# Weight loads of a two-branch kernel issued from ScalarE's DMA queue in place of SyncE's

## The chip, the cores and the metric

The kernel runs on one core of a Trainium2 chip. A core has TensorE for matmuls, VectorE (DVE), ScalarE (ACT) and GpSimd (POOL) for elementwise work, and SyncE (SP), which here only issues DMAs. Each engine takes its own instructions in order; engines wait for each other by semaphores. DMAs are issued as instructions of an engine's stream, here SyncE's and ScalarE's, and 16 DMA engines move the bytes. The metric is device microseconds of one execution.

## The reference

Both branches start from the same layer norm of x (2048 tokens of 448), and their sum is added to x:

```
xn = layernorm(x)
out = x + A(xn) + B(xn)
A: q, k, v = xn @ wqkv               (16 heads of 28)
   phi(t) = [softmax(t @ w_phi), softmax(-(t @ w_phi))]     for q and k, per head
   o = phi(q) @ (phi(k)^T v) / (phi(q) . sum(phi(k)) + 1e-6)
   A = o @ wo
B: h  = gelu(layernorm(xn) @ w1)     (448 columns in four groups)
   hs = [h shifted by 1, -1, 2, -2 tokens, group by group] @ w2
   x1 = xn + hs
   B  = x1 + gelu(layernorm(x1) @ w3) @ w4      (448 -> 1792 -> 448)
```

All tensors are bfloat16.

## The kernel before

Tokens are cut into 16 tiles of 128. The contraction of 448 is laid out in pieces of 64 rows, so that two matmuls run at once on the two row halves of TensorE.

The kernel is recorded as a flat list of operations. `Recorder.op` (L67) takes an engine, an output and inputs; `solve` (L76) derives from the order of the list which operation has to wait for which; `emit` (L152) writes one in-order stream for each engine. So the order of an engine's instructions is the order in which the list names them, and all operations have the lines of the recorder's helpers in the profile: L204 matmuls, L208 transposing matmuls, L212 ScalarE activations, L216 elementwise work, L219 transposing DMAs, L222 plain DMAs. `R.dma` (L221) and `R.dma_t` (L218) have SyncE as their default issuer.

The order is written by hand in two lists:

- A chain (L944 to L967) covers the front: layer norm of all tiles, its transposition to xnT, the V products (`ZV`), the w1 products with Gelu (`ZW`, `ZR`), the folding of w_phi into the q and k weights (`FO`), and the first pair of k, w2 and q products (`HF`). It interleaves matmuls of the two row halves; an entry `do(...)` is put into the list just where it stands, while the eviction belonging to a matmul group comes when the group's last matmul is placed.
- A play list (L1034 to L1057) covers the rest: k products with exponentials (`k0`, `k1`), q products (`q0`, `q1`), w2 products (`w0`, `w1_`), transpositions of the q exponentials (`T`) and of the second layer norm (`G`), the sum over keys (`K`), the w3 products with Gelu (`a`, `b`), the attention quotient (`N`) and the last products with w4 and wo (`f`), with stores (`S`).

The DMAs around the change are:

- `h_shift(0)` and `h_shift(1)` (L668): six copies each inside the tile hT, which put the shifted upper rows of h in place; w2 products read them.
- `rest_T(0)` and `rest_T(1)` (L665): transposition of the last 64 columns of h from hR (which shares its memory with gT, so the profile names it gT) to hRT. `rest_out` (L662) is the Gelu on ScalarE that writes hR.
- `load_w2` (L389): three DMAs, 336 KB and twice 56 KB. `load_w4` (L397): one of 1568 KB. `load_w3` (L394): two halves of 896 KB, called at two places. `wo_in` (L1030): two of 224 KB into the tile wv, which the V products have finished with by then. In the profile w1, w2, w3 and w4 are all named w.
- `q_T` (L706): 16 transpositions from hi, the q exponentials, to eqT. The lower eight land in eqT_lo, the upper eight in the memory of hT. `g_T` (L746): 16 transpositions from g_tok to gT.

ScalarE evicts most of PSUM in the front and all of the k and q exponentials (phik and hi) and the Gelus (hT, gT in the front; phik in the w3 stage, where h3T shares its memory). It changes its function table at the end of the front, before the first exponential, and again before the first Gelu of the w3 stage. At the start ScalarE's queue issues five loads, of x, wv and w1, beside SyncE's; at the end one store.

Of the kernel before, what the change touches and what calls it, by code (L numbers as in the profile page):

```python
# [6 lines left out]
ACT = mybir.ActivationFunctionType  # L7
# [217 lines left out]
def bass_parallel_sum__linear_kernel_hedgehog__mixer_s_mlp__prompt_kernel(  # L225
# [17 lines left out]
    with es:  # L243
# [249 lines left out]
        def fold(t, m, b, n):  # L493
            def side(k, hi):
                r, c0, c1 = (slice(64, CR), 2 * DH, CR) if hi else (slice(0, 64), 0, 3 * DH)
                return [(banks[b + k][:, CR * c + c0:CR * c + c1],
                         wT[r, t, c, START[m + k]:START[m + k] + 128], bd[r, CR * c + c0:CR * c + c1], n == 0 and c == 0)
                        for c in range(NC)]
            return side(n, 0), side(1 - n, 1)
# [24 lines left out]
        def xn_Td(i):  # L524
            R.dma_t(xnT[:, :, 128 * i:128 * i + 128], xn[:, i, :])
# [8 lines left out]
        def halves_of(first, second, start=False):  # L534
            return tuple([(out, lhs, rhs, start and n == 0) for n, (out, lhs, rhs) in enumerate(side)] for side in (first, second))
# [99 lines left out]
        def z_w1(g, m, b):  # L635
            def make(rows, kcs):
                lo, hi = rows
                return [(banks[b], w1[lo:hi, kc, 128 * m:128 * m + 128], xnT[lo:hi, kc, 512 * g:512 * g + 512],
                         rows == LO and n == 0) for n, kc in enumerate(kcs)]
            return make  # L640
# [230 lines left out]
        def play(fs):  # L871
            for f in fs:
                f[0](*f[1:])
# [18 lines left out]
        def do(f, *args):  # L892
            return "do", lambda: f(*args), ()
# [4 lines left out]
        def FO(t, m, n):  # L898
            return "both", fold(t, m, fb[t, m], n), ((fold_out, t, m, fb[t, m]),) if n else ()

        def XT(i, b, n=1, eng="ACT"):
            return "both", xn_T(i, b, n), ((xn_out, i, b, n, eng),)

        def XD(*t):
            return do(lambda: [xn_Td(i) for i in t])
# [4 lines left out]
        def ZV(i, *then):  # L910
            return "zip", z_v(i, vb[i]), then

        def ZW(g, m, *then):
            return "zip", z_w1(g, m, gb[g][m]), then
# [4 lines left out]
        def inside(n, job, inner):  # L919
            return (*job, (n, inner))  # L920

        def ZR(h, b, *then):
            return "zip", z_rest(h, b), then

        def EV(i, eng="ACT", n=1):
            return v_out, i, vb[i], eng, n

        def EW(g, m, n):
            return w1_out, g, m, gb[g][m], n
# [6 lines left out]
        def HF(p, n):  # L936
            then = ((), ((k_exp, 0, kq[0][0], 0), (k_exp, 0, kq[0][0], 1)), ((w2_out, 0, wb[0]),),
                    ((q_exp, 0, kq[0][1], 0), (q_exp, 0, kq[0][1], 1)))[(p + 1) * n]
            return "half", halves_of(*head[p][n], n == 0), then
# [20 lines left out]
            XT(8, 1, 1, "ACT"), ZW(3, 2, EW(3, 2, 1)), L(("r", 9, 1)), FO(1, 2, 0), L(("a", 10)), FO(1, 0, 1),  # L960
            ZW(3, 1, EW(3, 1, 1)), FO(1, 2, 1), ZV(12, EV(12, "DVE", 1)), ZV(8, EV(8, "DVE", 1)), L(("p", 9)),
            inside(3, ZR(0, 6, (rest_out, 0, 6), (rest_T, 0)), XT(9, 3, 1, "2")), FO(0, 2, 0),
            FO(0, 0, 0), XD(10), FO(0, 2, 1), FO(0, 0, 1), do(h_shift, 0), ZW(2, 2, EW(2, 2, 1)), do(load_w2),
            ZR(1, 5, (rest_out, 1, 5)), ZW(2, 1, EW(2, 1, 1)), ZV(11, EV(11, "ACT", 1)), ZV(10, EV(10, "ACT", 1)),
            ZW(2, 0, EW(2, 0, 1)), ZV(9, EV(9, "DVE", 1)), do(kv_picks), HF(0, 0), do(late_3), do(kv_ones), HF(1, 0), HF(2, 0),
            do(load_w4), do(h_shift, 1), do(rest_T, 1), HF(0, 1), do(load_w3, 0), HF(1, 1), HF(2, 1)], 400,
            "001010111100101001010010111010100")  # L967

        kp = [phi_pair(wpk, 2 * n, kq[n][0]) for n in range(8)]
# [53 lines left out]
        def f(n, k):  # L1023
            fp[k][n - 1]()
# [5 lines left out]
        def wo_in(eng="SP"):  # L1030
            load_lap(wo, A_wo, (eng, eng))

        K, G, S, T, kc, kb, W = kv_tile, g_T, store, q_T, kv_turn, kv_blocks, fin_tails
        play([  # L1034
            (w0, 2), (lo, 0), (kn, 0), (load_w3, 1), (k0, 1), (kx, 0), (k0, 2), (k1, 1), (w1_, 2), (q0, 1), (k1, 2),
            (q1, 1), (q0, 2), (T, 0), (k0, 3), (kn, 1), (q1, 2), (kn, 2), (T, 1), (lo, 1), (kx, 1), (kx, 2), (w0, 4),
            (k1, 3), (w1_, 4), (q0, 3), (k0, 4), (kn, 3), (q1, 3), (k1, 4), (w0, 6), (T, 3), (q0, 4), (w1_, 6),
            (lo, 3), (q1, 4), (kx, 3), (lo, 2), (sc, 0), (K, 0), (K, 1), (K, 2), (K, 3), (k0, 5), (q0, 5), (k1, 5),
# [2 lines left out]
            (A, 0), (lo, 6), (w1_, 10), (k1, 7), (kx, 4), (kx, 5), (lo, 4), (w0, 12), (lo, 5), (q0, 7), (w1_, 12),  # L1041
            (sc, 4), (lo, 11), (G, 0), (kn, 6), (A, 7), (AD, 4), (G, 2), (kn, 7), (A, 6), (T, 8), (lo, 10), (q1, 7),
            (a, 0), (w0, 14), (b, 0), (a, 1), (w1_, 14), (A, 5), (b, 1), (a, 2), (kx, 6), (K, 9), (K, 6), (a, 3),
            (wo_in,), (T, 10), (b, 2), (G, 6), (G, 4), (b, 3), (K, 13), (kx, 7), (lo, 9), (lo, 8), (G, 5), (K, 12),
            (K, 8), (K, 11), (lo, 15), (a, 4), (a, 5), (b, 4), (b, 5), (lo, 13), (K, 7), (K, 14), (lo, 14), (K, 15),
            (G, 7), (K, 10), (kc,), (sc, 8), (a, 6), (kb,), (T, 9), (a, 7), (A, 9), (b, 6), (A, 10), (N, 0), (b, 7),
            (f, 1, 0), (N, 1), (a, 9), (AD, 8), (AD, 11), (T, 11), (G, 11), (a, 8), (G, 9), (b, 9), (b, 8), (N, 2),
# [44 lines left out]
```

## Time and profile before

| | |
|---|---|
| three runs, median | 173.2 us (171.03 to 173.53) |
| profiled execution | 170.78 us, span of its instructions 169.1 us |
| DMA | 19.93 MB in 50567 packets, mean 118 GB/s |
| SyncE's DMA queue (q1) | 18.71 MB, 56.9% of the 16 engines' span |
| ScalarE's DMA queue (q10) | 0.89 MB, 1.6% |
| granted TensorE clock | 1.00 throughout |

The span runs from the first to the last instruction. "Busy" of TensorE is modelled for pipelined matmuls, so neighbouring matmuls overlap in the rows. A row of a timeline has the start, the length, the engine ("q" behind it for an instruction of its queue, a DMA issue), the line, the operation, the tiles (out<-in), the shapes and the count, and in brackets the idle time of the engine before it with what ended it. A row of DMA issues ends with the size and the time from issue to landing.

### The profile page before, as it was taken

To read this page: it belongs to the slowest core of one execution; us is meant where nothing else is said; L and a number is where in the kernel's file an instruction comes from. 1 tells how busy PE (TensorE), PEld (TensorE's weight loads), DVE (VectorE), ACT (ScalarE), POOL (GpSimd) and SP (SyncE) were. 2 spreads that over 40 slices of the span, in tenths; PEclk is the share of its full clock that TensorE was granted. 3 is DMA by queue.
4 is the path that set the end of the run, shared out by engine and by line. 5 is a ranking of instruction groups with operands and counts; after the bars stand their busy time and mean duration, and the time that the engine had idled before them with its cause. 6 is when DMAs were issued, how large, how long until landed. Compare 5 with 4: busy or idle time off the path is not lost.

```text
span 169.1 us, 5415 instructions
## 1 busy us (share of the span) xinstructions
PE 165.2 (98%) x2355; PEld 92.9 (55%) x2355; DVE 110.2 (65%) x250; ACT 79.4 (47%) x107; POOL 91.5 (54%) x125
## 2 busy tenths in 40 slices
PE   8899999999999999999999999999999999999994
PEld 7587679755455444445554555555455555444453
DVE  3889968149999989996692952876228656250131
ACT  3499873867997887555142422222042202504000
POOL 5578891003999999993645472272602717234040
PEclk9999999999999999999999999999999999999999
DMA  5995444699999959573026761467592113214011
GB/s 163 335 222 101 77 55 97 161 345 184 395 204 197 137 108 155 99 90 68 17 49 124 97 124 38 104 107 123 135 108 58 35 31 33 51 52 128 0 54 54
DMA packets 50567, 19.93 MB, mean 118 GB/s; under 512 B 41712, under 2 KB 49840, under 8 KB 50544
## 3 DMA queue, kind: packets, MB, share of 16 engines
q1 hardware_dynamic: 49424, 18.71, 56.9%
q10 hardware_dynamic: 1120, 0.89, 1.6%
q8 instruction: 18, 0.29, 0.7%
q14 instruction: 5, 0.04, 0.1%
HBM read 7.14 MB, written 1.84 MB: 53 GB/s over the span
## 4 chain that ended last, share of the span: by engine, by line
PE 98%; ACT 0%; DVE 0%; issue 0%
PE banks L204 96%; PE banks L208 1%; ACT xnT L212 0%; DVE vaug L216 0%; ACT rs L212 0%
## 5 line engine op out<-in xcount | busy, mean ns | idle before, releaser
L212 ACT ACTIVATE phik<-banks 128x1024 bf16<-128x1024 f32 (+1 forms) x44 | 41.7, 987 | 63.2 <-PE banks L204 63.2
L204 PE MATMUL banks<-gT,w 64*128 64x512 bf16 x392 | 47.1, 376 | 0.0
L204 PE MATMUL banks<-w,phik 64*128 64x448 bf16 (+3 forms) x434 | 45.2, 343 | 0.0
L216 DVE TENSOR_TENSOR vaug<-banks,vaug 128x464 f32<-128x464 f32 (+3 forms) x65 | 32.6, 511 | 19.2 <-PE banks L204 17.5
L216 POOL TENSOR_TENSOR xnT<-vaug 128x196 bf16<-128x196 f32 (+1 forms) x32 | 18.2, 589 | 40.8 <-DVE vaug L216 40.8
L721 POOL TENSOR_TENSOR phik<-phik,rks 128x1792 bf16<-128x1792 bf16 x8 | 25.6, 3216 | 15.1 <-DVE rks L216 15.1
L204 PE MATMUL banks<-wv,xnT 64*128 64x448 bf16 (+2 forms) x222 | 33.2, 346 | 0.0
L204 PEld LDWEIGHTS banks<-w,phik 64*128 64x128 bf16 (+1 forms) x434 | 22.2, 94 | 19.9 <-issue 0.4
L204 PEld LDWEIGHTS banks<-gT,w 64*128 64x128 bf16 x392 | 18.0, 94 | 19.8 <-ACT phik L212 1.5
L216 POOL TENSOR_TENSOR vaug<-xn,xtok 128x448 f32<-128x448 bf16 x16 | 16.2, 1034 | 8.2 <-DVE vaug L216 8.2
L216 DVE RECIPROCAL vaug<-banks 128x16 f32<-128x16 f32 x16 | 4.1, 256 | 23.0 <-PE banks L204 23.0
L204 PEld LDWEIGHTS banks<-wv,xnT 64*128 64x128 bf16 (+1 forms) x222 | 14.3, 94 | 7.8 <-ACT xnT L212 0.6
L204 PE MATMUL banks<-xnT,w 64*128 64x512 bf16 (+1 forms) x105 | 17.5, 333 | 0.0
L216 DVE TENSOR_REDUCE ksum<-phik 128x64 f32<-128x1792 bf16 x8 | 15.9, 1991 | 0.0
L212 ACT ACTIVATE hi<-banks 128x896 bf16<-128x896 f32 x16 | 13.7, 928 | 1.4 <-PE banks L204 1.4
L204 PE MATMUL banks<-wpk,xnT 64*128 64x448 bf16 x112 | 14.4, 350 | 0.0
L204 PE MATMUL banks<-wpq,xnT 64*128 64x448 bf16 x112 | 14.0, 349 | 0.0
L204 PE MATMUL banks<-w,hT 64*128 64x448 bf16 x96 | 13.0, 349 | 0.0
L216 DVE TENSOR_TENSOR xn<-banks,xn 128x512 bf16<-128x512 f32 (+1 forms) x16 | 9.0, 605 | 3.2 <-PE banks L204 3.1
L216 DVE BATCH_NORM_STATS2 st<-xtok 128x6 f32<-128x448 bf16 x16 | 9.7, 607 | 0.5 <-DMA xtok<-in_A_x_dram 0.5
L216 POOL TENSOR_TENSOR rs<-mv,mhalf 128x1 f32<-128x1 f32 (+1 forms) x13 | 9.3, 719 | 1.0 <-DVE mv L216 1.0
L216 DVE BATCH_NORM_STATS2 st<-xn 128x6 f32<-128x448 bf16 x16 | 9.5, 591 | 0.0
(63 smaller groups left out, 158.5 us busy)
## 6 DMA issues: line engine op xcount, KB each, us to landing
w<-in_B_w_dram SPq DMA_DIRECT2D x2, 896.0 KB, 7.2
out_dram<-vaug SPq DMA_DIRECT2D x15, 112.0 KB, 1.9
w<-in_B_w_dram SPq DMA_DIRECT2D x1, 1568.0 KB, 9.2
xtok<-in_A_x_dram SPq DMA_DIRECT2D x2, 448.0 KB, 6.7
wv<-in_A_wo_dram SPq DMA_DIRECT2D x2, 224.0 KB, 4.2
xtok<-in_A_x_dram SPq DMA_DIRECT2D x3, 112.0 KB, 3.9
xtok<-in_A_x_dram ACTq DMA_DIRECT2D x3, 112.0 KB, 4.1
w<-in_B_w_dram SPq DMA_DIRECT2D x1, 336.0 KB, 4.0
```

What stands on the lines that cost most here:

```text
L204: self.op("PE", lambda e: e.matmul(out, lhsT, rhs, start=start, stop=stop, skip_group_check=True), [out], [lhsT, rhs], tile=self._tile(lhsT))
L208: self.op("PE", lambda e: e.transpose(out, in_, ident), [out], [in_, ident], tile=self._tile(in_))
L212: self.op("ACT", lambda e: e.activation(out, in_, func, **kw), [out], [in_] + aps)
L216: self.op(eng, lambda e: getattr(e, name)(out, *args, **kw), [out], aps)
L721: R.op(pool, lambda e: e.tensor_tensor(ph, ph, wide, op=ALU.mult), [ph], [ph, wide, *after])
```

## The change

Eight DMA issues move from SyncE's stream to ScalarE's, each at the place in the recorded order where it stood. The helpers already took the issuing engine as an argument and are not changed.

```diff
-            FO(0, 0, 0), XD(10), FO(0, 2, 1), FO(0, 0, 1), do(h_shift, 0), ZW(2, 2, EW(2, 2, 1)), do(load_w2),
+            FO(0, 0, 0), XD(10), FO(0, 2, 1), FO(0, 0, 1), do(h_shift, 0), ZW(2, 2, EW(2, 2, 1)), do(load_w2, "ACT"),
...
-            do(load_w4), do(h_shift, 1), do(rest_T, 1), HF(0, 1), do(load_w3, 0), HF(1, 1), HF(2, 1)], 400,
+            do(load_w4, "ACT"), do(h_shift, 1), do(rest_T, 1), HF(0, 1), do(load_w3, 0, "ACT"), HF(1, 1), HF(2, 1)], 400,
...
-            (w0, 2), (lo, 0), (kn, 0), (load_w3, 1), (k0, 1), (kx, 0), (k0, 2), (k1, 1), (w1_, 2), (q0, 1), (k1, 2),
+            (w0, 2), (lo, 0), (kn, 0), (load_w3, 1, "ACT"), (k0, 1), (kx, 0), (k0, 2), (k1, 1), (w1_, 2), (q0, 1), (k1, 2),
...
-            (wo_in,), (T, 10), (b, 2), (G, 6), (G, 4), (b, 3), (K, 13), (kx, 7), (lo, 9), (lo, 8), (G, 5), (K, 12),
+            (wo_in, "ACT"), (T, 10), (b, 2), (G, 6), (G, 4), (b, 3), (K, 13), (kx, 7), (lo, 9), (lo, 8), (G, 5), (K, 12),
```

In ScalarE's stream the three loads of w2 now stand between the xnT copy and the first Gelu of the rest block; w4 and the first half of w3 between the last Gelu of hT and the change of the function table; the second half of w3 between the first q exponentials and the k exponentials behind them; wo between the second and the third Gelu of the w3 stage. SyncE's stream is the same without them. The streams of TensorE, VectorE and GpSimd are the same.

## The prediction

> **What bounds the kernel now.** I read the page first: its span, the busy times, the slices and the chain that ended last.
>
> ```profile
> span 169.1 us, 5415 instructions
> PE 165.2 (98%) x2355; PEld 92.9 (55%) x2355; DVE 110.2 (65%) x250; ACT 79.4 (47%) x107; POOL 91.5 (54%) x125
> ...
> PE 98%; ACT 0%; DVE 0%; issue 0%
> ```
>
> TensorE is busy for 165.2 of 169.1 us and 98% of the last chain is its own. A gain has to come out of the 3.9 us in which it idles, or out of a matmul stream that looks dense and is not. The second view, busy time by stretch, covers the place of the moved loads (columns: length, then busy us and count for PE, PE weight loads, DVE, ACT, POOL, then clock, DMA share, GB/s).
>
> ```profile
> 28.00:32.00 4.00, 4.00 (x64) 3.31 (x61) 1.35 (x10) 3.15 (x6) 0.00 (x0) 1.00 0.59 157
> 32.00:36.00 4.00, 3.90 (x43) 2.31 (x41) 0.62 (x1) 2.47 (x4) 0.00 (x0) 1.00 0.83 232
> 40.00:44.00 4.00, 4.00 (x46) 2.03 (x42) 3.97 (x6) 3.83 (x6) 3.21 (x1) 1.00 1.13 262
> 44.00:48.00 4.00, 4.00 (x46) 2.01 (x42) 3.93 (x7) 3.99 (x5) 3.87 (x2) 1.00 1.11 354
> ```
>
> Only the stretch from 32 us shows a hole in TensorE, 0.10 us of idle. From 40 to 48 us TensorE, VectorE and ScalarE are all full and the DMA share is above 1: anything that makes ScalarE late there has little to absorb it. The clock is 1.00 throughout, so nothing in the sum depends on it. The timelines of the weight loads and of TensorE show what made the hole.
>
> ```profile
> 33.11 0.09 PEld L204 LDWEIGHTS banks<-w,hRT 64*128 64x128 bf16 x1 [0.52 <-issue]
> 37.21 1.82 PEld L204 LDWEIGHTS banks<-wpk,xnT 64*128 64x128 bf16 x22 [0.36 <-ACT phik L212]
> 32.69 0.35 PE L204 MATMUL banks<-wpk,xnT 64*128 64x448 bf16 x1
> 33.14 0.35 PE L204 MATMUL banks<-w,hRT 64*128 64x448 bf16 x1
> ```
>
> The first matmul that uses hRT starts 0.45 us after the one before it, where the 43 matmuls of that stretch come on average every 4.00/43 = 0.09 us. The view names no engine for that wait. SyncE's timeline and the list of DMA issues give the likely one:
>
> ```profile
> 23.52 4.42 SPq L222 DMA_DIRECT2D hT<-hT  x6
> 27.98 2.31 SPq L222 DMA_DIRECT2D w<-in_B_w_dram  x3
> 30.34 1.27 SPq L219 DMA_TRANSPOSE hRT<-gT  x1
> 31.65 0.58 SPq L222 DMA_DIRECT2D w<-in_B_w_dram  x1
> 32.75 3.74 SPq L222 DMA_DIRECT2D hT<-hT  x6
> 36.53 1.36 SPq L219 DMA_TRANSPOSE hRT<-gT  x1
> 37.93 2.09 SPq L222 DMA_DIRECT2D w<-in_B_w_dram  x2
> 63.09 1.11 SPq L222 DMA_DIRECT2D wv<-in_A_wo_dram  x2
> ...
> hRT<-gT SPq DMA_TRANSPOSE x1, 2.7
> ```
>
> The transposition of hRT's first half is issued at 30.34 and lands 2.7 us later, at 33.04; the weight load that needs it starts at 33.11. So the hole is, by coincidence of times, a DMA that stood behind the three w2 loads on SyncE.
>
> **What leaves SyncE.** Eight DMA issues: w2 in three (2.31 us), w4 (0.58), w3 in two (2.09), wo in two (1.11), together 6.09 us of issue time. Only the w2 part stands ahead of something TensorE waited for. ScalarE's activations, where its queue will now hold these issues, are:
>
> ```profile
> 25.16 0.39 ACT L212 ACTIVATE xnT<-banks 128x256 bf16<-128x256 bf16 x1
> 27.73 0.60 ACT L212 ACTIVATE gT<-banks 128x512 bf16<-128x512 f32 x1 [2.18 <-PE banks L204]
> 32.13 0.60 ACT L212 ACTIVATE hT<-banks 128x512 bf16<-128x512 f32 x1
> 32.74 1.28 ACT L212 ACT_TABLE_LOAD   x1
> 35.44 1.73 ACT L212 ACTIVATE phik<-banks 128x896 bf16<-128x896 f32 x2 [1.41 <-PE banks L204]
> 37.05 1.73 ACT L212 ACTIVATE hi<-banks 128x896 bf16<-128x896 f32 x2
> 39.51 0.92 ACT L212 ACTIVATE phik<-banks 128x896 bf16<-128x896 f32 x1 [0.73 <-PE banks L204]
> 71.72 1.94 ACT L212 ACTIVATE phik<-banks 128x1024 bf16<-128x1024 f32 x2 [1.80 <-PE banks L204]
> ```
>
> The Gelu of the rest block that hRT's transposition reads is the gT activation at 27.73, done at 28.33. SyncE has finished the six shifts at 23.52 + 4.42 = 27.94. Without the w2 loads the transposition starts at about 28.35 instead of 30.34, 2.0 us sooner, and lands at 28.35 + 2.7 = 31.05. TensorE wants it at about 32.8: the hole closes, worth 0.45 − 0.1 = 0.35 to 0.45 us; I take 0.4. If, with w2's rows now coming from another queue at the same time, it takes 6.2 us as its second half did,
>
> ```profile
> hRT<-gT SPq DMA_TRANSPOSE x1, 6.2
> ```
>
> it lands at 34.55, and the hole grows by 1.5 us instead. I take the 2.7, because w2 is issued some 2.4 us earlier too and is mostly through by then, and the DMA share from 28 to 32 us is only 0.59.
>
> **What comes to ScalarE.** Its program order becomes: the xnT copy, three w2 issues, the gT Gelu; then after the hT Gelu of 32.13 w4 and the first half of w3, the table load, the first pair of exponentials; the second half of w3 after the hi pair of 37.05; wo after the second Gelu of the last stage, before that of 71.72. None of the eight waits for anything (w2, w3, w4 are first written here, and the tile of wo was last read by the V products, which end before the stretch from 36 us), so a late semaphore cannot hold the queue. What they cost is their issue time, against the idle time in front of the next activation:
>
> w2: the gap is 27.73 − 25.55 = 2.18 us, the price 2.31 at SyncE's rate. At worst the gT Gelu is 0.13 us late, and the transposition behind it has 1.7 us in hand. Nothing.
>
> w4 and the first half of w3: between the hT Gelu's end (32.73) and the exponential at 35.44 lie 2.71 us, of which the table load takes 1.28. The issues cost 0.58 + about 0.5 = 1.1 (the two w3 issues took 2.09 together), leaving 0.3 us. With TensorE 0.4 earlier the exponential could start at 35.04; ScalarE is ready at 32.73 + 1.1 + 1.28 = 35.1. That is a draw. From below: ScalarE's queue can issue while the engine works, as it did at the start, where a table load ran beside four issues that cost 0.38 to 0.49 each:
>
> ```profile
> 0.79 1.28 ACT L365 ACT_TABLE_LOAD   x1 [0.79 <-PEq L1077]
> 0.82 0.38 ACTq L222 DMA_DIRECT2D xtok<-in_A_x_dram  x1
> 1.74 0.98 ACTq L222 DMA_DIRECT2D xtok<-in_A_x_dram  x2
> ```
>
> Then the pair is paid beside the hT Gelu and ScalarE is ready at 34.5. From above: the slower of the two w3 issues took 1.56,
>
> ```profile
> 37.93 1.56 SPq L222 DMA_DIRECT2D w<-in_B_w_dram  x1
> ```
>
> and with it ScalarE is ready at 32.73 + 0.58 + 1.56 + 1.28 = 36.15, 0.7 late; TensorE waits for just this eviction at 37.21, so that would be passed on. I take the draw, nearest to how ScalarE's own issues ran.
>
> Second half of w3: 0.73 us of idle stand before 39.51, the issue is 0.5 to 1.56. Zero at the low price, 0.8 late at the high one, and here the rows from 40 us have no slack. I take zero. wo: 1.80 us of idle against 1.11. Zero, or 0.4 if each issue took 1.1.
>
> What is queued behind a late issue is always the next eviction of PSUM, and who waits is TensorE, for the bank.
>
> **What SyncE does with 6.1 us less.** The second half's shifts start when the Gelu of 32.13 ends, as before; the eqT and gT transpositions behind them can start one to two microseconds sooner. No row of TensorE's waits names them, so this gains nothing in sight.
>
> **A rule of the skill beside it.** The Trainium skill, in "DMA: Bandwidth & Descriptors", section "Issuing engines are not separate DMA queues", says that spreading issues over engines buys only sequencer time, since all run on the same 16 DMA engines. This agrees with the DMA share above 1 from 40 to 48 us, where a second queue can add no bytes, and by it too the gain is no more than the one wait behind w2's issues.
>
> **The sum.** Stall −0.4, ScalarE 0 (bounds 0 and +0.7 + 0.8 + 0.4 = 1.9), transposition late 0 (bound +1.5 + 0.4). The profiled execution took 170.78 us in all, 1.7 more than its span: it becomes 170.4. The three runs gave 173.2 as median, from 171.03 to 173.53, so the profiled one lies at their fast end; on the median's level the forecast is 173.2 − 0.4 = 172.8 us.
>
> **The rivals.**
>
> *A full queue holds ScalarE.* SyncE showed that an issue can wait for what stands in its queue: this transposition, behind the 1.8 MB of w3, took 4.07 us against 1.27 for the one at 30.34.
>
> ```profile
> 42.80 4.07 SPq L219 DMA_TRANSPOSE eqT_lo<-hi  x1
> w<-in_B_w_dram SPq DMA_DIRECT2D x1, 1568.0 KB, 9.2
> ```
>
> On ScalarE the first half of w3 comes straight behind the 1568 KB of w4. Held for 4.07 us from 33.31, ScalarE is free at 37.4, through the table load at 38.7, 3.2 us after 35.44; held until w4 lands, 32.73 + 9.2, it is 7.8 late. TensorE has banks until 37.2 and then stands still. Middle: 5.5, so 173.2 + 5.5 = 178.7 us. It passes 2% (3.5 us) from a w3 issue of about 4.3 us on. Against it: SyncE's shift at 32.75, also straight behind w4, paid 3.74/6 = 0.6. Chance 0.21.
>
> *Small exposed costs.* ScalarE's bounds half met, or hRT late by the 1.5: +0.5 to +2.3, near 174.4 us. For it: the full stretch from 40 us. Chance 0.11.
>
> *Hidden anyway.* The hole closes and the table load or the next eviction gives it back: 173.2 us. For it speaks the wait at 37.21. Chance 0.13.
>
> *The spread goes.* If the longer of the three runs are longer because w2 or hRT lands late there, the change gives that transfer 2 us of reserve, and all runs come out near 171.03 − 0.4 = 170.6. No trace shows one of the longer runs, so this has 0.14. It is 1.5% alone; only with the kernel before at its high end (173.53) and a little more does it pass 2%.
>
> **How the numbers follow.** The forecast itself has 0.41. 2% is about what a measurement of this kernel can tell from no change; it lies at 169.7 and 176.7. Slower is the full queue, 0.21. Faster is some two thirds of the case of the spread, 0.09. The rest is 0.70. The predicted time is 172.8. The range begins at 170.2, the profiled execution's level with the hole closed and 0.2 to spare, and reaches to 176.4, the near end of the full queue, 173.2 + 3.2; what it leaves out is most of that rival.
>
> **What would show it.** Right: in the trace after, hRT's transposition issues near 28.4, the weight load near 32.8 has no wait before it, the first phik exponential starts between 35.0 and 35.5, and ScalarE's eight issues take 0.4 to 0.6 each. Wrong: a ScalarE issue of over 1.5 us, an exponential after 36, or new waits of TensorE's weight loads for ScalarE between 37 and 56 us. An execution that is faster by over 1 us would say that something behind SyncE's transpositions mattered that no wait of this trace names.

## The result and the profile after

| | before | after |
|---|---|---|
| median of 20 runs | 171.72 us (170.84 to 173.53) | 173.01 us (172.40 to 173.84) |
| ratio, 95% interval | | 1.0082 [1.0058, 1.0105] |
| profiled execution | 170.78 us, span 169.1 | 173.84 us, span 172.1 |

The change costs 0.8%, or 1.3 us, where 0.4 us of gain was forecast. The profiled execution of the changed kernel is at the upper end of its runs, so its trace shows the loss large. Ratios use fast runs alone, so they need not be the quotient of the medians; in the repeat of the change below this leaves out three runs of 173.2 to 174.6 us. The page of the changed kernel, the span and the chain that ended last:

```profile
span 172.1 us, 5415 instructions
...
PE 72%; DVE 12%; POOL 8%; DMA 5%; issue 1%; ACT 0%; SPq 0%
PE banks L204 71%; DVE ksum L216 5%; POOL phik L721 4%; DMA xnT<-xn 3%; DMA gT<-g_tok 2%; DVE xn L216 2%; DVE st L216 2%; POOL rs L216 2%; POOL g_tok L216 2%; DVE rks L216 1%; POOL xn L216 1%; PE banks L208 1%; DVE mv L216 1%; DVE vaug L216 0%; DVE g_tok L216 0%
```

Before, TensorE held 98% of this chain. Now two DMAs are in it that were not: xnT<-xn and gT<-g_tok. TensorE's timeline shows where the second one ends:

```profile
64.70 0.73 PE L204 MATMUL banks<-wpq,xnT 64*128 64x448 bf16 x6
67.03 0.82 PE L204 MATMUL banks<-gT,w 64*128 64x512 bf16 x6 [1.60 <-DMA gT<-g_tok]
```

The first matmul of the w3 stage waits 1.6 us for a transposition of gT. In the kernel before, the same matmul followed without a gap:

```profile
64.34 1.03 PE L204 MATMUL banks<-gT,w 64*128 64x512 bf16 x8
```

ScalarE's timeline in the changed kernel, with the issues of w2, w4 and w3 in it as "ACTq" rows, shows whether the issues themselves cost anything:

```profile
25.43 1.83 ACTq L222 DMA_DIRECT2D w<-in_B_w_dram  x3
28.68 0.60 ACT L212 ACTIVATE gT<-banks 128x512 bf16<-128x512 f32 x1 [2.87 <-PE banks L204]
...
33.02 0.60 ACT L212 ACTIVATE hT<-banks 128x512 bf16<-128x512 f32 x1
33.03 1.40 ACTq L222 DMA_DIRECT2D w<-in_B_w_dram  x2
34.52 1.28 ACT L212 ACT_TABLE_LOAD   x1 [0.91 <-issue]
36.05 1.73 ACT L212 ACTIVATE phik<-banks 128x896 bf16<-128x896 f32 x2 [0.24 <-PE banks L204]
37.19 0.37 ACTq L222 DMA_DIRECT2D w<-in_B_w_dram  x1
```

They cost nothing that is passed on. The table load stands 0.91 us behind the two issues, and the exponential behind it still waits 0.24 us for TensorE. What matters is the start of the second ACTq row: w4 is issued at 33.03, with the hT Gelu that stands ahead of it in ScalarE's order, where SyncE issued it at 31.65. SyncE's timeline and the list of DMA issues of the changed kernel:

```profile
29.31 1.52 SPq L219 DMA_TRANSPOSE hRT<-gT  x1
33.65 3.78 SPq L222 DMA_DIRECT2D hT<-hT  x6
37.47 1.33 SPq L219 DMA_TRANSPOSE hRT<-gT  x1
39.42 19.37 SPq L219 DMA_TRANSPOSE eqT_lo<-hi  x8
58.84 5.22 SPq L219 DMA_TRANSPOSE gT<-g_tok  x4
...
hRT<-gT SPq DMA_TRANSPOSE x1, 11.6
...
eqT_lo<-hi SPq DMA_TRANSPOSE x1, 10.5
...
gT<-g_tok SPq DMA_TRANSPOSE x1, 4.1
```

The same two rows of the kernel before, and its landings of the first eqT and the fourth gT:

```profile
40.06 16.35 SPq L219 DMA_TRANSPOSE eqT_lo<-hi  x8
56.46 5.22 SPq L219 DMA_TRANSPOSE gT<-g_tok  x4
...
eqT_lo<-hi SPq DMA_TRANSPOSE x1, 7.8
...
gT<-g_tok SPq DMA_TRANSPOSE x1, 2.5
```

SyncE comes to the eqT transpositions 0.6 us sooner and leaves them 2.4 us later (39.42 + 19.37 = 58.79 against 40.06 + 16.35 = 56.41). hRT's second half, issued at 37.47, takes 11.6 us where it took 6.2. The four gT issues start 2.4 us later, and the fourth takes 4.1 us to land instead of 2.5. Before, it landed at about 62.9, 1.4 us ahead of its matmul at 64.3; after, at 66.9.

### The profile page after: what moved, and what is told of

Same layout as the page of the kernel before. It is cut to its first block, busy times and chain, and to the rows that moved or that the text cites. A ratio compares the mean times of both kernels' runs of the same rounds, so it can differ in the third digit from the quotient of the medians.

```text
span 172.1 us, 5415 instructions
## 1 busy us (share of the span) xinstructions
PE 166.2 (97%) x2355; PEld 100.4 (58%) x2355; DVE 110.5 (64%) x250; ACT 79.4 (46%) x107; POOL 91.2 (53%) x125
## 4 chain that ended last, share of the span: by engine, by line
PE 72%; DVE 12%; POOL 8%; DMA 5%; issue 1%; ACT 0%; SPq 0%
PE banks L204 71%; DVE ksum L216 5%; POOL phik L721 4%; DMA xnT<-xn 3%; DMA gT<-g_tok 2%; DVE xn L216 2%; DVE st L216 2%; POOL rs L216 2%; POOL g_tok L216 2%; DVE rks L216 1%; POOL xn L216 1%; PE banks L208 1%; DVE mv L216 1%; DVE vaug L216 0%; DVE g_tok L216 0%
## 5 line engine op out<-in xcount | busy, mean ns | idle before, releaser
L204 PE MATMUL banks<-gT,w 64*128 64x512 bf16 x392 | 47.7, 376 | 1.6 <-DMA gT<-g_tok 1.6
L216 POOL TENSOR_TENSOR xnT<-vaug 128x196 bf16<-128x196 f32 (+1 forms) x32 | 18.2, 588 | 40.9 <-DVE vaug L216 40.9
L204 PEld LDWEIGHTS banks<-w,phik 64*128 64x128 bf16 (+1 forms) x434 | 25.2, 94 | 17.0 <-issue 0.4
L204 PEld LDWEIGHTS banks<-gT,w 64*128 64x128 bf16 x392 | 20.5, 94 | 19.4 <-issue 2.0
L204 PEld LDWEIGHTS banks<-wv,xnT 64*128 64x128 bf16 (+1 forms) x222 | 15.1, 94 | 7.1 <-ACT xnT L212 0.6
```

Source lines behind the costliest of these rows:

```text
L204: self.op("PE", lambda e: e.matmul(out, lhsT, rhs, start=start, stop=stop, skip_group_check=True), [out], [lhsT, rhs], tile=self._tile(lhsT))
L216: self.op(eng, lambda e: getattr(e, name)(out, *args, **kw), [out], aps)
```

## The experiments

The first four tell apart three causes: weights that start late, two queues that share the DMA engines, and ScalarE's issue time.

**w2 alone.** The edit, against the kernel before:

```diff
-do(load_w2),
+do(load_w2, "ACT"),
```

> Only the three w2 loads are on ScalarE, all else as before. Late weights (the change lets the bulk of the weights start 1.4 us later, at 33.03 instead of 31.65, so that all transpositions behind them land later and the first w3 matmul waits for gT): no loss here, w4 starts near 30 us, the first gT matmul runs at 64.3 or a little sooner, time 0 to -0.4 us against before. Two queues (transpositions lose their turns to weight rows in another queue): no loss either, since w2 is through by 31 us. ScalarE's issues exposed: at most +0.2 us.

Measured: 170.73 us, 0.9959 [0.9934, 0.9985] of before. SyncE's and TensorE's timelines, with the landing of the fourth gT:

```profile
28.33 1.37 SPq L219 DMA_TRANSPOSE hRT<-gT  x1
...
64.19 1.02 PE L204 MATMUL banks<-gT,w 64*128 64x512 bf16 x8
...
gT<-g_tok SPq DMA_TRANSPOSE x1, 2.5
```

hRT's first half is issued at 28.33, as forecast, and the weight load that used to wait for it does not wait. TensorE's timeline has the first matmul on hRT 0.4 us sooner than the kernel before, which had it at 33.14:

```profile
32.73 0.35 PE L204 MATMUL banks<-w,hRT 64*128 64x448 bf16 x1
```

That is the 0.4 us of the prediction. By the ratio the run gains 0.4%, or 0.7 us, with an interval of 0.3 to 1.1 us.

**w4 and w3 alone.**

```diff
-do(load_w4),
+do(load_w4, "ACT"),
-do(load_w3, 0),
+do(load_w3, 0, "ACT"),
-(load_w3, 1),
+(load_w3, 1, "ACT"),
```

> Only w4 and the two halves of w3 are on ScalarE; w2 and wo stay on SyncE. Late weights and two queues alike: the whole loss is here, +1.0 to +1.8 us against before, a wait of 1 to 2.5 us before the first gT matmul, the last of the first four gT transpositions landing after 65 us. ScalarE's issues exposed: +0.6 us, seen as a first phik exponential after 35.9 that waits for the table load and not for TensorE.

Measured: 172.83 us, 1.0084 [1.0057, 1.0112]. TensorE's timeline has the wait, and the fourth gT takes as long as in the full change:

```profile
66.55 1.04 PE L204 MATMUL banks<-gT,w 64*128 64x512 bf16 x8 [1.55 <-DMA gT<-g_tok]
...
gT<-g_tok SPq DMA_TRANSPOSE x1, 4.3
```

So the loss sits with w4 and w3, though w4 is issued only 0.6 us later here than in the kernel before (32.25 against 31.65). The first exponential ran at 35.93 behind 0.95 us of waiting for TensorE: ScalarE's issue time is not the cause.

**w4 late, one queue.** In the kernel before, SyncE issues w4 behind the second shifts:

```diff
-do(load_w4), do(h_shift, 1), do(rest_T, 1),
+do(h_shift, 1), do(load_w4), do(rest_T, 1),
```

> All loads on SyncE as before, but w4 is issued behind the second six shifts, at about 36 us instead of 31.65. Late weights: the DMA engines idle for some 4 us, the eqT transpositions land 3 to 4 us later, the first gT matmul waits 2 to 3 us, +2 to +3.5 us. Two queues: a single queue serves all, so no change, within 0.3 us. ScalarE's issues exposed: no change.

Measured: 174.95 us, 1.022 [1.0199, 1.0241], or 3.8 us by the ratio, a little over the 2 to 3.5 us expected. Its list of waits:

```profile
ACT hi L212 <- DMA eqT_lo<-hi: 1.8, 1, 1.8
PE banks L204 <- issue: 1.7, 1, 1.7
```

The first is an exponential that waits until eqT has been read out of the buffer it writes; the second stands before the first gT matmul, at 68.32. The fourth gT takes 4.3 us here too. Here w4 starts 5.7 us late (37.34), far more than in the change, so the sizes are not to be compared; but a wait at gT needs no second queue when w4 starts late.

**w4 early, two queues.** The changed kernel, w4 directly behind w2:

```diff
-do(load_w2, "ACT"),
+do(load_w2, "ACT"), do(load_w4, "ACT"),
-do(load_w4, "ACT"), do(h_shift, 1),
+do(h_shift, 1),
```

> The changed kernel with w4 issued directly behind w2 on ScalarE, at about 27 us instead of 33. Late weights: the weights are through some 3 us sooner, the wait before the first gT matmul is gone, the time is that of before or up to 0.4 us under it. Two queues: SyncE's transpositions still share with ScalarE's rows; the loss of about 1.3 us stays or grows, and the first hRT transposition lands after 33 us. ScalarE's issues exposed: half of the loss stays, as w3's half is still issued ahead of the table load.

Measured: 176.68 us, 1.0328 [1.0291, 1.0365]. Late weights alone had this wrong. The waits and the issue of hRT's first half:

```profile
PE banks L204 <- DMA hRT<-gT: 3.5, 1, 3.5
...
hRT<-gT SPq DMA_TRANSPOSE x1, 8.1
```

Beside w4's rows on the other queue the transposition takes 8.1 us instead of 2.7 and TensorE stands for 3.5. A queue of its own did not take the transposition past the large load. The wait before gT is absent, but everything ahead of it is late, so this run says nothing of that wait.

**w4 at its old start, two queues.** The changed kernel with w4 two instructions earlier on ScalarE, ahead of the last V eviction and the last hT Gelu, when hRT's first half has been under way for 2.3 us:

```diff
-ZW(2, 0, EW(2, 0, 1)), ZV(9, EV(9, "DVE", 1)),
+ZW(2, 0, EW(2, 0, 1)), do(load_w4, "ACT"), ZV(9, EV(9, "DVE", 1)),
-do(load_w4, "ACT"), do(h_shift, 1),
+do(h_shift, 1),
```

> The changed kernel with w4 issued one place earlier on ScalarE, between the last two V evictions, near 31 us, so that its rows start no later than in the kernel before, while hRT's first half has landed. Late start: the second hRT half and eqT land as before (first eqT by 48.3), no wait before the first gT matmul, 0.994 to 0.999 of before. Two queues: the second hRT half still lands only after most of w3, after 46 us, the first eqT after 49, and 1.004 or more of before remains.

Measured: 170.94 us, 0.9942 [0.9905, 0.9980]. ScalarE, SyncE and TensorE in its timelines, and the landings of the first eqT and the fourth gT:

```profile
31.64 0.37 ACTq L222 DMA_DIRECT2D w<-in_B_w_dram  x1
39.43 17.89 SPq L219 DMA_TRANSPOSE eqT_lo<-hi  x8
57.36 5.22 SPq L219 DMA_TRANSPOSE gT<-g_tok  x4
64.96 1.03 PE L204 MATMUL banks<-gT,w 64*128 64x512 bf16 x8
...
eqT_lo<-hi SPq DMA_TRANSPOSE x1, 8.5
...
gT<-g_tok SPq DMA_TRANSPOSE x1, 2.5
```

One load, moved ahead of one eviction and one Gelu, turns +0.8% into −0.6%. w4 starts at 31.64, eqT lands at 47.9 as in the kernel before, and no wait stands before gT. All eight loads are still on ScalarE, and w3's first half is issued at 33.04, about as early as in the change (33.45; 37.93 in the kernel before), so its early start is not the loss. hRT's second half again landed only with the end of w3 (issued at 37.42, landed at 46.98); no wait of TensorE names it. The busy time from 32 to 34 us, in the kernel before, in the changed one and in this one, shows what a late w4 leaves unused (the last two columns are the DMA share and GB/s):

```profile
32.00:34.00 2.00, 1.90 (x21) 1.15 (x19) 0.62 (x1) 1.88 (x3) 0.00 (x0) 1.00 0.60 116
...
32.00:34.00 2.00, 2.00 (x24) 1.40 (x22) 0.41 (x1) 1.31 (x3) 0.00 (x0) 1.00 0.00 0
...
32.00:34.00 2.00, 2.00 (x24) 1.39 (x22) 0.40 (x1) 1.67 (x4) 0.00 (x0) 1.00 0.55 97
```

**w4 out of the way.** Two runs put w4 into the w3 stage, one with the rest of the change, one with w2 alone:

```diff
-(b, 4), (b, 5), (lo, 13),
+(b, 4), (b, 5), (load_w4, "ACT"), (lo, 13),
-do(load_w4, "ACT"), do(h_shift, 1),
+do(h_shift, 1),
```

> The changed kernel with w4 issued on ScalarE in the w3 stage, behind the second b(5), near 80 us, instead of at 33: 1.57 MB leave the time in which the eqT transpositions run. Late transpositions (the weights on ScalarE's queue hold up hRT and eqT, these hold up gT on SyncE): eqT's first lands before 45 us, the last of the first four gT lands before 63.5, no wait before the first gT matmul, hole before hRT closed too: 0.994 to 0.998 of before. ScalarE's issues exposed: w3's half still stands ahead of the table load and wo and w4 among the Gelus, so 1.002 or more.

> Only w2 and w4 on ScalarE, w4 near 80 us; w3 and wo on SyncE as before. Late transpositions: as in the run before it, 0.993 to 0.997 of before, since w3 alone is too little to hold up anything on either queue. If the two differ by over 0.3%, the queue of w3 matters by itself and two queues side by side cost something that the sum of bytes does not.

Measured: 178.14 us, 1.0355 [1.0296, 1.0415], and 178.03 us, 1.0346 [1.0284, 1.0408]. The waits of the first:

```profile
PE banks L204 <- DMA w<-in_B_w_dram: 5.1, 1, 5.1
```

I had put the load too late: w4's first use is near 80 us, and TensorE waited 5 us for it. Neither run says anything of the time; the first gT matmul of the first one, at 64.49, did start without a wait. Another run gave w4 time enough, behind the last q exponentials, with w2 on ScalarE and w3 and wo on SyncE:

> Only w2 and w4 on ScalarE; w4 is issued behind the last q exponentials, near 66 us, early enough for its first use near 80. If the weights in front of the second hRT half and eqT are what makes gT late, the last of the first four gT lands before 63, nothing waits for it, w4 lands before 77, and the time is 0.993 to 0.997 of before. If two queues side by side cost something of their own, the gT and eqT transpositions of 62 to 76 us take 4 us or more each and the time is 1.0 or more.

Measured: 170.98 us, 0.999 [0.9959, 1.0021]. No wait at gT and no hole at hRT, and yet less gain than the expected 0.993 to 0.997. Beside w4 (issued at 64.55) three transpositions took 5.1 to 6.0 us where the kernel before took 2.5 and 3.2, as the second reading expected, but TensorE's timeline has no wait of over 0.1 us from 8 us on. Its front is 0.3 us later than with w2 alone (first exponential at 35.43 against 35.13). What took the rest I did not find.

**Why the fourth gT takes 4.1 us.** In the traces where it does, a packet of queue q8, which the page calls "instruction", falls into it. The rows of the changed kernel from 62.8 to 67 us:

```profile
q1 hardware_dynamic: 1542, 0.38, 74.9%
q8 instruction: 1, 0.02, 1.7%
```

In the kernel before that packet came just behind the fourth gT and into the next transposition, hT<-hi at 61.72, which took 4.9 us. To move the packet without touching a DMA (it went from 64.16 to 67.40 in the changed kernel), the changed kernel and the kernel before were run with fewer TensorE instructions at the start:

```diff
-        spin(30)
+        spin(10)
```

> The changed kernel with 10 instead of 30 dummy matmuls at the start, so that the 16 KB reads of queue q8, which come about every 9 us and of which one falls on 64.1 us in each profile, move some 40 TensorE instructions later, 1 to 2 us at that place. Read in the way (the last gT transposition takes 4.1 us instead of 2.5 because that read falls into it, and only this makes TensorE wait): the transposition lands 2.5 us after its issue, the wait before the first gT matmul is under 0.5 us, the time 0.997 to 1.002 of before. Late transpositions alone: the wait stays at 1 us or more and the time at 1.006 to 1.010. If the clock or the front suffers from fewer dummies, it shows before 20 us and is taken off.

> The kernel before with 10 dummy matmuls at the start instead of 30: what the front alone loses by it. Read in the way: this kernel loses all that the changed one lost by the same step and its gain of no wait, so that the changed kernel with 10 dummies (1.011 of before) is within 0.4% of it, 1.008 to 1.013 here. Late transpositions alone: the change keeps its 0.8% with 10 dummies too, so this one is at 1.001 to 1.005.

Measured: the changed kernel with 10 dummies 173.88 us, 1.011 [1.005, 1.017] of before; the kernel before with 10 dummies 173.71 us, 1.0135 [1.0103, 1.0168]. The first one's timelines, and the landing of the fourth gT:

```profile
40.55 18.15 SPq L219 DMA_TRANSPOSE eqT_lo<-hi  x8
66.33 1.03 PE L204 MATMUL banks<-gT,w 64*128 64x512 bf16 x8
...
gT<-g_tok SPq DMA_TRANSPOSE x1, 2.5
```

Fewer dummies make the front late, and not equally: the first exponential runs at 37.18 in the changed kernel with 10 dummies and at 38.86 in the kernel before with 10, where it ran at 36.05 and 35.44 with 30. So both are slower, and the quotient of the two ratios, 0.998 with intervals of 0.6% and 0.3%, does not show by itself that the change costs nothing. The traces leave the front out: from the first exponential to the end, the kernel before takes 133.6 us with 30 dummies and 133.6 with 10, the changed kernel 136.1 with 30 (135.2 in the second profile below) and 134.0 with 10.

The eqT transpositions still hold SyncE for 18.2 us in the first of these runs, against 16.4 in the kernel before and 19.4 and 18.8 in the two profiles of the change. Yet the fourth gT, issued at 63.51, lands after 2.5 us and nothing waits; with the 4.1 us of the change it would have landed 1.3 us after 66.33 (an estimate). The time I expected for the first run (0.997 to 1.002) did not take the front's loss into account; the wait, as expected, is gone. The second run's 1.0135 lies just above the 1.008 to 1.013 of the reading with the packet and far from the 1.001 to 1.005 of lateness alone, but the unequal front has a part in it.

**The change once more.**

> The changed kernel again, for a second profile. If the wait before the first gT matmul is the loss, it is 1 to 2 us again, with the last of the first four gT landing 4 us or more after its issue, beside the read of queue q8 near 64 us; the time is 1.005 to 1.011 of before. If the longer stretch before hRT or the front makes the loss, the wait varies and the front is late again by more than 0.5 us at the first phik exponential.

Measured: 172.39 us, 1.0035 [1.0002, 1.0067]. The timelines of ScalarE and TensorE, and the landing:

```profile
35.41 1.73 ACT L212 ACTIVATE phik<-banks 128x896 bf16<-128x896 f32 x2 [0.25 <-PE banks L204]
65.88 1.04 PE L204 MATMUL banks<-gT,w 64*128 64x512 bf16 x8 [1.39 <-issue]
...
gT<-g_tok SPq DMA_TRANSPOSE x1, 4.0
```

The front runs as in the kernel before (first exponential at 35.41 against 35.44), and the wait is there again. So the wait does not need the late front of the first profile of the change, where TensorE waited for xnT near 27 us; the run with w4 at its old start has the same late front in its trace (first exponential at 36.06) and no wait. The time is below the 1.005 to 1.011 that I expected, and less than half of the first measurement's loss. Four of the twelve runs took 170.4 to 171.3 us, like the kernel before; no trace shows one of them.

## Why the prediction was wrong

- *The hole at hRT, −0.4 us: right.* hRT's first half went out at 28.3 with w2 alone and at 29.3 in the change, as soon as its Gelu was done, and the hole closed. With w2 alone the first matmul on hRT came 0.4 us sooner.
- *ScalarE's issues, 0: right, and the draw too.* They took 0.37 to 0.99 us each, and the exponential behind the table load still waited 0.24 us for TensorE.
- *"The eqT and gT transpositions behind them can start one to two microseconds sooner": this step failed.* The prediction costed the eight moved issues at their issue time and let the bytes flow as before. But a load that leaves SyncE's place also leaves the time at which SyncE issued it. On ScalarE w4 goes out only when the Gelu ahead of it starts, 0.7 us (32.39 in the second profile) to 1.4 us later. The DMA share from 32 to 34 us falls from 0.60 to 0.00 (0.25 in the second profile), and from 36 to 48 us it is 0.98 or more in all three, so what was not moved then pushes back what follows. The last shift, w3, hRT and eqT all end later, and gT behind them.
- *"No row of TensorE's waits names them": true, and no reason.* gT had 1.4 us in hand. Being 1.3 to 2.4 us late used that up and moved the fourth transposition onto the q8 packet, which added 1.6 us. It takes both, as an estimate from the issue times shows. With 2.5 us for the fourth gT it would have landed at 65.3 in the change, where TensorE came free at 65.4, and at 64.2 in the second profile, where it came free at 64.5: no wait. With 4.1 us in the kernel before it would have landed at 64.5 for a matmul at 64.3: a wait of 0.2 us. The sum had no term for the slack of a transfer that nobody waits for yet.
- *The full queue: right as a mechanism, at the wrong queue.* The first eqT issue in the change took 6.12 us. It held SyncE, not ScalarE; the kernel before had 2.69 and then 4.07 us there.
- *The small costs exposed* (+0.5 to +2.3 us) had the size of the result, from other causes. *The spread:* w2 alone ran from 170.38 to 171.57 us beside 170.49 to 175.18 of the kernel before; whether hRT's wait made that spread no trace shows.
- *The level.* The forecast stood on a median of three runs, 173.2; over 20 runs it is 171.72. That 172.8 lies beside the measured 173.01 comes from this and not from the argument.

The late start as cause is shown by the two runs that move w4 alone, one to a loss and one out of it. That the q8 packet makes the fourth gT slow is shown by coincidence in every trace that has the slow one (four) and by the run that moved the packet. No run separates how much of the loss each would make without the other; the estimate above says next to nothing each. Why the loss is 0.8% in one measurement and 0.35% in the other stays open.

## What to carry to other kernels

When a load moves to another engine's queue, ask first when that engine's order lets it start, and what the DMA engines do at that time; its issue time comes second. Take the slack of every transfer behind it from the trace before (landing against first use), also where nothing waits today. Here all eight loads on ScalarE gained after all, with w4 ahead of one more eviction and the last Gelu: 0.9942 of before. w2 alone, at 0.9959, is the same within the intervals, so moving the other loads gained nothing that these runs show.

## What the runs showed of the hardware

- One 16 KB packet of queue q8 (0.29 MB in 18 packets) stretched the fourth gT transposition from 2.5 to between 4.0 and 4.3 us in the four traces where it met it; in the changed kernel with 10 dummies it met the first, which took 3.6. The Trainium skill, "Runtime: NRT & Kernel Launch", section "Terms", says that an engine's instruction memory is refilled in blocks of 16 KiB. The traces agree in size, and moving TensorE's instruction count moved the packets, so these are most likely its refills.
- A transposition on SyncE's queue beside large loads on ScalarE's took 8.1 us where it took 2.7 in the kernel before, behind w2's small loads, and in the change hRT's second half took 11.6. Two queues did not let the small one pass.
- A DMA issue can hold its engine for 6.12 us: the first eqT transposition on SyncE, with the shifts and hRT's second half ahead of it on that queue, of which the last landed at 49.1. ScalarE's loads took under 1 us each, also the second half of w3 with w4 and the first half still under way.
